# Attention backward on one core: K transposed by the DMA crossbar in place of TensorE

## The chip, the cores and the metric

The kernel runs on one core of a Trainium2 chip. Time is the device time of one launch in microseconds (us), taken over several runs; the profile is of one execution. The core has five engines that run side by side and wait for one another by semaphores: TensorE (PE in the profile; PEld are its weight loads), VectorE (DVE), ScalarE (ACT), GpSimd (POOL) and SyncE (SP, which here only issues DMAs). Transfers between HBM and SBUF, the on-chip memory of 128 partitions, run on 16 DMA engines. TensorE writes to PSUM, eight banks that DVE and ACT read.

## The reference

Two independent blocks, A and B, of multi-head attention over a given cache of keys and values, forward and backward. B = 8 batches, Sq = 96 queries, D = 640, H = 32 heads, Sk = 512 keys, Dh = 128; all bf16.

```python
def ref(x, k_cache, v_cache, wq, wo):              # once for A, once for B
    q = (x @ wq).reshape(B, Sq, H, Dh).transpose(0, 2, 1, 3)
    scores = einsum("bhqd,bhkd->bhqk", q, k_cache) * (Dh ** -0.5)
    p = softmax(scores, axis=-1)
    o = einsum("bhqk,bhkd->bhqd", p, v_cache)
    return o.transpose(0, 2, 1, 3).reshape(B, Sq, H * Dh) @ wo

out, vjp = jax.vjp(lambda *a: concatenate([ref(*a[:5]), ref(*a[5:])], -1), *inputs)
return out, *vjp(grad_out)     # gradients of x, k_cache, v_cache, wq, wo of A and B
```

The caches and their gradients are by far the largest arrays: 8 x 32 x 512 x 128 values each, for K, V, dK and dV of A and of B.

## The kernel before

The work is cut into **cells**: one head h and one batch b of one block, 2 x 32 x 8 = 512 of them. A cell brings in K and V of its head and batch (512 keys x 128, 128 KB each), and sends out dK and dV of the same size. Around the cells lies work per head (projections of Q and of the output gradient, `pA` to `pD`, and the gradients of wq and wo, `qA` to `qD`) and work per group of eight heads (`gU`, L480: output and dx summed over heads).

Every step is a function that is put on a list with a **tick** and a slot within the tick (`em.add`). Cell number n starts at tick n, and each of its steps has a fixed offset in ticks from there (`OFF`, L45). The list is sorted by tick and slot, and the steps are emitted in that order; a planner then orders the instructions on each engine, mostly as emitted. The steps S2 and S3 (scores, softmax) are under `tc.high_priority(2000)` and are placed earlier, as soon as what they read is there. Tiles have a fixed number of buffers (`bufs=`); an instruction that writes a tile waits until the last reader of the buffer is through.

The steps of a cell, with their ticks before the change:

- `c_ld` (tick 0): two DMAs from SP's queue load K_sb (11 buffers) and V_sb (8). Partition p gets keys 4p to 4p+3 (KC = 4 of them, 1 KB in one piece), so column block c of a tile holds keys 4p + c.
- `c_s1` (tick 2): TensorE transposes the four blocks of K and the four of V (L243, L245) into one PSUM bank, DVE copies the 1024 columns to SBUF as KVT (L247, 5 buffers); KT and VT are its halves.
- `c_s2a`, `c_s2b` (tick 3): scores S = Q K^T (L259), their maximum (DVE, L261), the exponential E with its row sum (ACT, L271).
- `c_s3a`, `c_s3b` (tick 3): reciprocal (L281) and P = E / sum (POOL, L290; 5 buffers).
- `c_s4`, first part of `c_s45` (tick 4): dV = P^T dO (L330), its copy (ACT, L332) to dV_sb (3 buffers), its store from SP's queue (L333); P transposed on TensorE (L313).
- second part of `c_s45` (tick 5): O^T = V^T P^T, which reads natural V (L306).
- `c_s6` (tick 6): dP = dO V^T, which reads VT (L352), and dS (DVE, L356).
- `c_s7`, first part of `c_s78` (tick 7): dK = dS^T Q (L394), its copy (ACT, L396) to dK_sb (3 buffers) and store (L397); dS transposed (L377).
- second part of `c_s78` (tick 8): dQ^T, which reads natural K (L370).

Natural K is thus read at ticks 2 and 8, natural V at ticks 2 and 5, KT at 3, VT at 6. The keys stand in the order (c, p) in every tile with a key axis; dS and P use the same order as the natural tiles, since they are multiplied with them.

Of the kernel before, what the change touches and what calls it, by code (L numbers as in the profile page):

```python
# [7 lines left out]
ACT = mybir.ActivationFunctionType  # L8
# [3 lines left out]
BF16 = mybir.dt.bfloat16  # L12
# [29 lines left out]
SL_GRP = 95  # L42
SL_SETUP = 96

OFF = dict(ld=0, s1=2, s2=3, s3=3, s4=4, s5=5, s6=6, s7=7, s8=8)  # L45
HK = dict(pA=-5, pB=-3, pC0=[-2, 0], pC1=[-1, 0], pD1=1, pD0=2, qA0=13, qA1=17, qB=[20, 17], qD=[(18, 0, 2), (19, 2, 5)])
EV = dict(pB0="act", pB1="dve", pC00="act", pC01="act", pC10="act", pC11="dve", pD0="dve", pD1="dve", qA0="dve", qA1="dve", qB0="act", qB1="act", qD="dve", gU="act")
GSPREAD0 = 9
# [2 lines left out]
SLOTS = dict(LOAD=0, S2A=5, S2B=5.5, S1=6, S8=10, S7=20, S5=30, S4=40, S6=50, S3A=52, S3B=53, S5B=54, HEAD=SL_HEAD, GRP=SL_GRP)  # L51


def build_block(tc, em, tick0, blk, x, kc, vc, wq, wo, g_all, out_all, dx, dk, dv, dwq, dwo, ident, ones, pools, HG=8, first=True, groups=None):
    nc = tc.nc
    B, Sq, D = x.shape
    _, H, Sk, Dh = kc.shape
# [5 lines left out]
    KC = Sk // 128  # L63
    scale = float(Dh) ** -0.5
# [27 lines left out]
    const, ps, kvp, wk, hd, hst, grp = (pools[k] for k in ("const", "ps", "kvp", "wk", "hd", "hst", "grp"))  # L92

    def bank(shape, dt, name):
        return ps.tile(shape, dt, name=name, tag="bank")
# [4 lines left out]
    CS = pools["CS"]  # L100
# [12 lines left out]
    def setup_T(which_, c):  # L113
        def f():
            key = "xT" if which_ == 0 else "gT"
            if c == 0:
                S[key] = const.tile([128, DC, T], BF16, name=key, bufs=1)
            dst = S[key]
            if first:
                tmp = S["x_nat" if which_ == 0 else "g_nat"][:, :, c * 128:(c + 1) * 128]  # L120
            else:
                tmp = S.pop(("tmp", which_, c))
            for t0 in range(0, TT, 8):
                nt = min(8, TT - t0)
                pt = bank([128, 8 * 128], BF16, "tp_ps")
                for i in range(nt):
                    nc.tensor.transpose(pt[:, i * 128:(i + 1) * 128], tmp[:, t0 + i, :], ident[:])
                nc.vector.tensor_copy(dst[:, c, t0 * 128:(t0 + nt) * 128], pt[:, 0:nt * 128])
        return f

    def setup_nat(which_):
        def f():
            key = "x_nat" if which_ == 0 else "g_nat"
            src_flat = x_flat if which_ == 0 else g_flat
            t_ = const.tile([128, TT, D], BF16, name=key, bufs=1)
            (nc.sync if first else nc.gpsimd).dma_start(t_[:], src_flat.rearrange("(t p) d -> p t d", p=128))
            S[key] = t_
        return f
# [6 lines left out]
    for c in range(DC):  # L145
# [4 lines left out]
        em.add(tick0 - 7 + c, SL_SETUP, setup_T(1, c))  # L150
    em.add(tick0 + (-11 if first else B + OFF["s5"] - 2), SL_LOAD, setup_nat(1))
    em.add(tick0 + (-12 if first else B + OFF["s8"] - 2), SL_LOAD, setup_nat(0))

# [9 lines left out]
    def pA(h):  # L163
        def f():
            wo_h = hd.tile([128, D], BF16, name="wo_h", bufs=1)
            nc.gpsimd.dma_start(wo_h[:], wo[h * 128:(h + 1) * 128, :])
            wq_h = hd.tile([128, DC, 128], BF16, name="wq_h", bufs=1)
            with nc.allow_non_contiguous_dma(reason="per-head wq slice"):
                nc.gpsimd.dma_start(wq_h[:], wq_v[:, :, h * 128:(h + 1) * 128])
            HS[(blk, h)] = dict(wo_h=wo_h, wq_h=wq_h)  # L170
        return f
# [54 lines left out]
                evac(EV["pD%d" % which], dst[:, b0 * 128:(b0 + nb) * 128], n_ps[:, 0:nb * 128])  # L226
        return f

    def c_ld(h, b):
        def f():  # L230
            K_sb = kvp.tile([128, KC, 128], BF16, name="K_sb", bufs=11)
            V_sb = kvp.tile([128, KC, 128], BF16, name="V_sb", bufs=8)
            nc.sync.dma_start(K_sb[:], kc[b, h].rearrange("(p c) d -> p c d", c=KC))
            nc.sync.dma_start(V_sb[:], vc[b, h].rearrange("(p c) d -> p c d", c=KC))
            CS[(blk, h, b)] = dict(K_sb=K_sb, V_sb=V_sb)
        return f

    def c_s1(h, b):
        def f():
            st = CS[(blk, h, b)]  # L240
            kvT_ps = bank([128, 2 * Sk], BF16, "kvT_ps")
            for c in range(KC):
                nc.tensor.transpose(kvT_ps[:, c * 128:(c + 1) * 128], st["K_sb"][:, c, :], ident[:])  # L243
            for c in range(KC):
                nc.tensor.transpose(kvT_ps[:, Sk + c * 128:Sk + (c + 1) * 128], st["V_sb"][:, c, :], ident[:])  # L245
            KVT = wk.tile([128, 2 * Sk], BF16, name="KVT", bufs=5)
            nc.vector.tensor_copy(KVT[:], kvT_ps[:])  # L247
            st["KT"] = KVT[:, 0:Sk]
            st["VT"] = KVT[:, Sk:2 * Sk]
        return f  # L250

    def c_s2a(h, b):
# [12 lines left out]
    def c_s2b(h, b):  # L265
        def f():
            with tc.high_priority(PRIO_OFF):
                st = CS[(blk, h, b)]
                E_sb = wk.tile([Sq, Sk], BF16, name="E_sb", bufs=2)
                rowsum = wk.tile([Sq, 1], F32, name="rowsum", bufs=3)  # L270
                nc.scalar.activation(E_sb[:], st["S_ps"][:], ACT.Exp, bias=st["negm"][:], scale=1.0, accum_out=rowsum[:])  # L271
                st["E_sb"], st["rowsum"] = E_sb, rowsum
                del st["S_ps"]
        return f
# [223 lines left out]
    for g in range(NG):  # L498
        h0 = GH0[g]
        for hh in range(groups[g]):  # L500
            h = h0 + hh
            c0t = tick0 + h * B
            em.add(c0t + HK["pA"], SL_LOAD, pA(h))
            em.add(c0t + HK["pB"], SL_HEAD, pB(h))
            for si in range(NTS):
                em.add(c0t + HK["pC0"][min(si, len(HK["pC0"]) - 1)], SL_HEAD, pC(h, 0, si))
                em.add(c0t + HK["pC1"][min(si, len(HK["pC1"]) - 1)], SL_HEAD, pC(h, 1, si))
            em.add(c0t + HK["pD1"], SL_HEAD, pD(h, 1))
            em.add(c0t + HK["pD0"], SL_HEAD, pD(h, 0))
            for b in range(B):  # L510
                ct = c0t + b
                em.add(ct + OFF["ld"], SLOTS["LOAD"], c_ld(h, b))
                em.add(ct + OFF["s1"], SLOTS["S1"], c_s1(h, b))
                em.add(ct + OFF["s2"], SLOTS["S2A"], c_s2a(h, b))
                em.add(ct + OFF["s2"], SLOTS["S2B"], c_s2b(h, b))
                em.add(ct + OFF["s3"], SLOTS["S3A"], c_s3a(h, b))
                em.add(ct + OFF["s3"], SLOTS["S3B"], c_s3b(h, b))
                em.add(ct + OFF["s5"], SLOTS["S5B"], c_s5b(h, b))
                em.add(ct + OFF["s4"], SLOTS["S4"], c_s4(h, b))
                S45.setdefault(ct + OFF["s5"], [None, None, None])[0] = (blk, h, b)  # L520
                S45.setdefault(ct + OFF["s4"], [None, None, None])[1] = (blk, h, b)
                S45.setdefault(ct + OFF["s6"], [None, None, None])[2] = (blk, h, b)
                S78.setdefault(ct + OFF["s8"], [None, None])[0] = (blk, h, b)
                S78.setdefault(ct + OFF["s7"], [None, None])[1] = (blk, h, b)
                em.add(ct + OFF["s6"], SLOTS["S6"], c_s6(h, b))
                em.add(ct + OFF["s7"], SLOTS["S7"], c_s7(h, b))
            em.add(c0t + HK["qA0"], SL_HEAD, qA(h, 0))
            for di in range(len(dsplits)):
                em.add(c0t + HK["qB"][min(di, len(HK["qB"]) - 1)], SL_HEAD + 1, qB(h, di))
            em.add(c0t + HK["qA1"], SL_HEAD, qA(h, 1))  # L530
            qd_parts = HK["qD"]
            for (k_, c_lo, c_hi) in qd_parts:
                if c_lo < DC:
                    em.add(c0t + k_, SL_HEAD + 2, qD(h, c_lo, min(c_hi, DC)))
        cLg = tick0 + (h0 + groups[g] - 1) * B + B - 1
        gs0 = max(3, (GSPREAD0 * groups[g]) // HG)
        gs1 = max(3, (GSPREAD1 * groups[g]) // HG)
        em.add(cLg + OFF["s5"] - 2, SL_LOAD, gW(g))
        subs = [(0, t, gi) for t in range(TT) for gi in range(len(gsplits))] + [(1, t, gi) for t in range(TT) for gi in range(len(gsplits))]
        n_out = TT * len(gsplits)  # L540
        for i, (which, t, gi) in enumerate(subs):
            if which == 0:
                tk = cLg + OFF["s5"] + 2 + (i * gs0) // n_out
            else:
                tk = cLg + OFF["s8"] + 2 + gs0 - 3 + ((i - n_out) * gs1) // n_out
            em.add(tk, SL_GRP, gU(g, which, t, gi))
# [119 lines left out]
```

## Time and profile before

| | us |
|---|---|
| median of 3 runs (lowest, highest) | 1850.45 (1850.15, 1851.11) |
| the profiled execution, its span | 1848.8 |
| TensorE busy | 1818.4 |
| VectorE busy | 1518.6 |
| ScalarE busy | 1434.4 |
| GpSimd busy | 777.9 |

The profile page gives for every engine its busy time, and for every group of instructions (a line of the kernel, an engine, an operation) the count, the busy time, the mean duration of one, and the idle time of the engine before them with what ended it. Durations on TensorE overlap, since its matmuls are pipelined; a mean duration there is not what one instruction takes of the queue. The chain of waits follows the work that ended last back from the end: at each step to the instruction that released it, or to the one before it on its engine. Two kinds of stretch alternate in the trace: some 147 us in which cells run with the work per head alone, and some 84 us in which the sums over a group of heads run between them.

### The profile page before, as it was taken

What the parts mean: (1) busy time and instruction counts of PE and PEld (TensorE: products, weight loads), DVE (VectorE), ACT (ScalarE), POOL (GpSimd) and SP (SyncE); (2) the same over time, 40 slices, a digit from 0 to 9 for tenths busy, and PEclk for the clock granted to TensorE, in tenths of its full rate; (3) what the DMA queues carried; (4) which work ended last, traced back from release to release, by engine and by line L of the source; (5) the groups of instructions that cost most, each with busy time, mean ns of one, the idle gap of its engine ahead of it and who ended that gap; (6) DMA issues with size and microseconds to landing.
All of it is one profiled execution on the core that took longest, in us unless ns stands there. A gap on an engine that the chain in (4) does not pass through costs nothing.

```text
span 1848.8 us, 69797 instructions
## 1 busy us (share of the span) xinstructions
PE 1818.4 (98%) x26595; PEld 1571.4 (85%) x26744; DVE 1518.6 (82%) x3309; ACT 1434.4 (78%) x4041; POOL 777.9 (42%) x1378
## 2 busy tenths in 40 slices
PE   6999999999999999999999999999999999999998
PEld 5888888888888888888888888888888888888887
DVE  5888867888788887888878887678887888878885
ACT  4888877888668886788767888788876788767882
POOL 4444433444334443345455444334433444333435
PEclk9999999999999999999999999999999999999999
DMA  7666654666546655566575665456655566555652
GB/s 229 196 193 202 192 162 149 199 195 193 164 148 194 201 183 165 159 191 205 186 229 173 196 194 184 160 167 198 192 175 164 171 196 199 159 165 176 201 168 84
DMA packets 316688, 335.32 MB, mean 181 GB/s; under 512 B 38368, under 2 KB 302048, under 8 KB 316352
## 3 DMA queue, kind: packets, MB, share of 16 engines
q1 hardware_dynamic: 296480, 270.53, 46.2%
q0 software_dynamic: 19872, 60.32, 10.7%
q8 instruction: 210, 3.44, 0.8%
q14 instruction: 126, 1.03, 0.2%
HBM read 171.57 MB, written 159.12 MB: 179 GB/s over the span
## 4 chain that ended last, share of the span: by engine, by line
PE 95%; POOL 2%; issue 1%; DVE 1%; DMA 1%; ACT 0%; POOLq 0%; SPq 0%; ACTq 0%
PE q_ps L210 11%; PE o_ps L480 10%; PE dV_ps L330 6%; PE kvT_ps L243 6%; PE kvT_ps L245 6%; PE dK_ps L394 6%; PE dP_ps L352 6%; PE S_ps L259 6%; PE dwq_ps L445 6%; PE dwo_ps L425 5%; PE optp_ps L313 5%; PE dq_dst_ps L377 5%; PE optp_ps L306 5%; PE dq_dst_ps L370 5%; PE n_ps L225 3%; PE nat_ps L410 2%
## 5 line engine op out<-in xcount | busy, mean ns | idle before, releaser
L290 POOL TENSOR_SCALAR P_sb<-E_sb,rinv 96x512 bf16<-96x512 bf16 x512 | 354.2, 692 | 780.5 <-DVE rinv L281 775.2
L271 ACT ACTIVATE E_sb<-S_ps,negm 96x512 bf16<-96x512 f32 x512 | 349.1, 682 | 291.2 <-DVE negm L261 288.1
L356 DVE SCALAR_TENSOR_TENSOR dS_sb<-dP_ps,dl_ps,P_sb 96x512 bf16<-96x512 f32 x512 | 383.3, 749 | 108.1 <-PE dl_ps L354 103.1
L247 DVE COPY KVT<-kvT_ps 128x1024 bf16<-128x1024 bf16 x512 | 350.0, 684 | 70.7 <-PE kvT_ps L245 69.0
L261 DVE TENSOR_REDUCE negm<-S_ps 96x1 f32<-96x512 f32 x512 | 347.6, 679 | 35.8 <-PE S_ps L259 30.1
L332 ACT ACTIVATE dV_sb<-dV_ps 128x512 bf16<-128x512 f32 x512 | 313.3, 612 | 0.0
L396 ACT ACTIVATE dK_sb<-dK_ps 128x512 bf16<-128x512 f32 x512 | 300.5, 587 | 15.7 <-PE dK_ps L394 12.9
L319 ACT ACTIVATE PT_sb<-optp_ps 128x384 bf16<-128x384 bf16 x512 | 253.4, 495 | 0.0
L245 PE MATMUL kvT_ps<-ident,V_sb 128*128 128x128 bf16 x2048 | 198.0, 219 | 0.0
L394 PE MATMUL dK_ps<-Qnat_h,dS_sb 96*128 96x128 bf16 x2048 | 197.9, 219 | 0.0
L243 PE MATMUL kvT_ps<-ident,K_sb 128*128 128x128 bf16 x2048 | 197.9, 219 | 0.0
L330 PE MATMUL dV_ps<-dOnat_h,P_sb 96*128 96x128 bf16 x2048 | 197.9, 219 | 0.0
L259 PE MATMUL S_ps<-KVT,QT_h 128*96 128x512 bf16 x512 | 193.8, 379 | 2.2 <-DVE KVT L247 1.9
L352 PE MATMUL dP_ps<-KVT,dOT_h 128*96 128x512 bf16 x512 | 195.2, 381 | 0.0
L342 POOL TENSOR_TENSOR prod<-OT_h,dOT_h 128x96 bf16<-128x96 bf16 x512 | 186.2, 364 | 19.4 <-ACT OT_h L316 14.4
L243 PEld LDWEIGHTS <-K_sb 128*128 128x128 bf16 x2048 | 147.3, 98 | 36.9 <-issue 1.9
L379 DVE COPY dST_sb<-dq_dst_ps 128x384 bf16<-128x384 bf16 x512 | 175.4, 343 | 1.8 <-PE dq_dst_ps L377 0.8
L313 PE MATMUL optp_ps<-ident,P_sb 96*128 96x96 bf16 x2048 | 171.6, 205 | 2.3 <-POOL P_sb L290 2.0
L377 PE MATMUL dq_dst_ps<-ident,dS_sb 96*128 96x96 bf16 x2048 | 172.1, 206 | 0.5 <-DVE dS_sb L356 0.4
L306 PE MATMUL optp_ps<-PT_sb,V_sb 128*128 128x96 bf16 x2048 | 172.1, 206 | 0.0
L370 PE MATMUL dq_dst_ps<-dST_sb,K_sb 128*128 128x96 bf16 x2048 | 170.7, 206 | 0.0
L445 PE MATMUL dwq_ps<-dQnat,x_nat 128*128 128x128 bf16 x1920 | 143.2, 219 | 0.0
(84 smaller groups left out, 3949.8 us busy)
## 6 DMA issues: line engine op xcount, KB each, us to landing
out_dram<-dV_sb SPq DMA_DIRECT2D x512, 128.0 KB, 2.0
out_dram<-dK_sb SPq DMA_DIRECT2D x512, 128.0 KB, 2.3
K_sb<-in_A_k_cache_dram SPq DMA_DIRECT2D x256, 128.0 KB, 2.4
V_sb<-in_A_v_cache_dram SPq DMA_DIRECT2D x256, 128.0 KB, 2.5
K_sb<-in_B_k_cache_dram SPq DMA_DIRECT2D x256, 128.0 KB, 2.4
V_sb<-in_B_v_cache_dram SPq DMA_DIRECT2D x256, 128.0 KB, 2.5
out_dram<-dwq_sb POOLq DMA_DIRECT2D x64, 160.0 KB, 3.0
out_dram<-dwo_sb POOLq DMA_DIRECT2D x64, 160.0 KB, 2.7
```

What stands on the lines that cost most here:

```text
L243: nc.tensor.transpose(kvT_ps[:, c * 128:(c + 1) * 128], st["K_sb"][:, c, :], ident[:])
L245: nc.tensor.transpose(kvT_ps[:, Sk + c * 128:Sk + (c + 1) * 128], st["V_sb"][:, c, :], ident[:])
L247: nc.vector.tensor_copy(KVT[:], kvT_ps[:])
L259: nc.tensor.matmul(S_ps[:], hs["QT_h"][:, tok], st["KT"], start=True, stop=True)
L261: nc.vector.tensor_reduce(negm[:], S_ps[:], axis=AX.X, op=ALU.max, negate=True)
L271: nc.scalar.activation(E_sb[:], st["S_ps"][:], ACT.Exp, bias=st["negm"][:], scale=1.0, accum_out=rowsum[:])
L290: nc.gpsimd.tensor_scalar(P_sb[:], st["E_sb"][:], st["rinv"][:], 0.0, op0=ALU.mult, op1=ALU.add)
L330: nc.tensor.matmul(dV_ps[:, c * 128:(c + 1) * 128], P_sb[:, c * 128:(c + 1) * 128], hs["dOnat_h"][:, b * 128:(b + 1) * 128], start=True, s ...
L332: nc.scalar.activation(dV_sb[:], dV_ps[:], ACT.Identity, scale=1.0)
L352: nc.tensor.matmul(dP_ps[:], hs["dOT_h"][:, tok], st["VT"], start=True, stop=True)
L356: nc.vector.scalar_tensor_tensor(dS_sb[:], dP_ps[:], dl_ps[:, 0:1], st["P_sb"][:], op0=ALU.subtract, op1=ALU.mult)
L394: nc.tensor.matmul(dK_ps[:, c * 128:(c + 1) * 128], dS_sb[:, c * 128:(c + 1) * 128], hs["Qnat_h"][:, b * 128:(b + 1) * 128], start=True, s ...
```

## The change

K^T no longer comes from TensorE. A DMA transpose on SP's queue loads K a second time and writes it transposed to SBUF as KT (6 buffers, tick 0). It reads K of a cell as 16 rows of 32 keys (8 KB each) and puts out, for each of the 128 values of a key, 32 groups of 16: column 16 g + r of KT is key 32 r + g. The scores thus have their keys in another order, and the exponential of L271 reads them back in the order (c, p) by a rearranged access: for each c and each of the 16 rows r, eight values with a step of 64. Its output, and all after it, stand in the order of before.

V is still transposed by TensorE, now alone (VT, 512 columns), at tick 4 in place of 2. Natural V and natural K are loaded for two batches at a time (256 KB in one DMA; V2 with 5 buffers at tick 1 of the even batch, K2 with 4 at tick 5). Natural K is now read by dQ^T alone.

```diff
-OFF = dict(ld=0, s1=2, s2=3, s3=3, s4=4, s5=5, s6=6, s7=7, s8=8)
+OFF = dict(ldT=0, ldV=1, ldK=5, s1=4, s2=3, s3=3, s4=4, s5=5, s6=6, s7=7, s8=8)
...
-    def c_ld(h, b):
-        def f():
-            K_sb = kvp.tile([128, KC, 128], BF16, name="K_sb", bufs=11)
-            V_sb = kvp.tile([128, KC, 128], BF16, name="V_sb", bufs=8)
-            nc.sync.dma_start(K_sb[:], kc[b, h].rearrange("(p c) d -> p c d", c=KC))
-            nc.sync.dma_start(V_sb[:], vc[b, h].rearrange("(p c) d -> p c d", c=KC))
-            CS[(blk, h, b)] = dict(K_sb=K_sb, V_sb=V_sb)
+    def c_ldT(h, b):
+        def f():
+            KT = kvp.tile([128, Sk // 16, 16], BF16, name="KT", bufs=6)
+            nc.sync.dma_start_transpose(KT[:], kc[b, h].rearrange("(r g) d -> r (g d)", r=16))
+            CS.setdefault((blk, h, b), {}).update(KT=KT[:].rearrange("d g r -> d (g r)"))
+        return f
+
+    def c_ldV(h, b):
+        def f():
+            V2 = kvp.tile([128, 2, KC, 128], BF16, name="V2", bufs=5)
+            nc.sync.dma_start(V2[:], vc[b:b + 2, h].rearrange("b (p c) d -> p b c d", c=KC))
+            for i in range(2):
+                CS.setdefault((blk, h, b + i), {}).update(V_sb=V2[:, i])
+        return f
+
+    def c_ldK(h, b):
+        def f():
+            K2 = kvp.tile([128, 2, KC, 128], BF16, name="K2", bufs=4)
+            nc.sync.dma_start(K2[:], kc[b:b + 2, h].rearrange("b (p c) d -> p b c d", c=KC))
+            for i in range(2):
+                CS.setdefault((blk, h, b + i), {}).update(K_sb=K2[:, i])
         return f
 
     def c_s1(h, b):
         def f():
             st = CS[(blk, h, b)]
-            kvT_ps = bank([128, 2 * Sk], BF16, "kvT_ps")
+            vT_ps = bank([128, Sk], BF16, "vT_ps")
             for c in range(KC):
-                nc.tensor.transpose(kvT_ps[:, c * 128:(c + 1) * 128], st["K_sb"][:, c, :], ident[:])
-            for c in range(KC):
-                nc.tensor.transpose(kvT_ps[:, Sk + c * 128:Sk + (c + 1) * 128], st["V_sb"][:, c, :], ident[:])
-            KVT = wk.tile([128, 2 * Sk], BF16, name="KVT", bufs=5)
-            nc.vector.tensor_copy(KVT[:], kvT_ps[:])
-            st["KT"] = KVT[:, 0:Sk]
-            st["VT"] = KVT[:, Sk:2 * Sk]
+                nc.tensor.transpose(vT_ps[:, c * 128:(c + 1) * 128], st["V_sb"][:, c, :], ident[:])
+            VT = wk.tile([128, Sk], BF16, name="VT", bufs=5)
+            nc.vector.tensor_copy(VT[:], vT_ps[:])
+            st["VT"] = VT[:]
         return f
...
-                nc.scalar.activation(E_sb[:], st["S_ps"][:], ACT.Exp, bias=st["negm"][:], scale=1.0, accum_out=rowsum[:])
+                nc.scalar.activation(E_sb[:].rearrange("q (c r s) -> q c r s", c=KC, r=16), st["S_ps"][:].rearrange("q (s c r) -> q c r s", c=KC, r=16), ACT.Exp, bias=st["negm"][:], scale=1.0, accum_out=rowsum[:])
...
-                em.add(ct + OFF["ld"], SLOTS["LOAD"], c_ld(h, b))
+                em.add(ct + OFF["ldT"], SLOTS["LOAD"], c_ldT(h, b))
+                if b % 2 == 0:
+                    em.add(ct + OFF["ldV"], SLOTS["LOAD"], c_ldV(h, b))
+                    em.add(ct + OFF["ldK"], SLOTS["LOAD"], c_ldK(h, b))
```

## The prediction

> **What bounds the kernel now.** I read the page first: its busy shares, then the chain that ended last.
>
> ```profile
> span 1848.8 us, 69797 instructions
> PE 1818.4 (98%) x26595; PEld 1571.4 (85%) x26744; DVE 1518.6 (82%) x3309; ACT 1434.4 (78%) x4041; POOL 777.9 (42%) x1378
> PE 95%; POOL 2%; issue 1%; DVE 1%; DMA 1%; ACT 0%; POOLq 0%; SPq 0%; ACTq 0%
> ```
>
> TensorE is busy in 98% of the span and is 95% of the chain, so what counts is how long its queue is and whether it ever stands still. How much a group of its instructions holds the queue is not their mean duration (219 ns, pipelined), but the step in the chain of waits in order of time (start, length, what):
>
> ```profile
> 804.97 0.22 PE kvT_ps L243 x4
> 805.19 0.22 PE kvT_ps L245 x4
> 805.41 0.17 PE dq_dst_ps L370 x4
> ```
>
> Four transposes of K (L243) take 0.22 us of the queue, and so do the four of V (L245). An average over the span mixes two stages, so I took a stretch of each. In the windows below the columns after the length are PE, PEld, DVE, ACT and POOL busy, granted clock, DMA share, GB/s; the second fence is the same two windows for the score matmul of L259 alone, whose count is the number of cells (one head and one batch).
>
> ```profile
> 314.00:461.00 147.00, 146.37 (x2228) 126.09 (x2238) 129.76 (x284) 126.33 (x359) 64.70 (x117) 1.00 0.62 195
> 461.00:545.00 84.00, 83.63 (x1163) 73.15 (x1169) 65.48 (x146) 53.52 (x147) 27.61 (x48) 1.00 0.49 154
> ```
>
> ```profile
> 314.00:461.00 147.00, 17.39 (x46) 5.60 (x46) 1.00 0.62 195
> 461.00:545.00 84.00, 7.21 (x19) 2.33 (x19) 1.00 0.49 154
> ```
>
> In the **plain stage** a cell takes 147/46 = 3.20 us, of which ACT works 126.33/46 = 2.75, DVE 129.76/46 = 2.82, and the DMA engines 0.62 x 3.20 = 1.98. In the **group stage** (the projections of L480 run between cells) it takes 84/19 = 4.42 us, ACT 2.82, DVE 3.45, DMA 0.49 x 4.42 = 2.17. The two windows are 231 us for 65 cells; 512 cells are 7.88 such periods, 1820 us, and the other 29 us are start and tail. TensorE stands still for 0.63 us of the 147, so it is the bound in both stages, at full granted clock (1.00).
>
> **The change, part by part.**
>
> *TensorE.* Of the eight transposes of a cell four go, with their weight loads: 0.22 us x 512 = 113 us off the queue. Nothing is added on it. What is late next is read below.
>
> *DVE.* The copy out of PSUM halves from 1024 to 512 columns.
>
> ```profile
> L247 DVE COPY KVT<-kvT_ps 128x1024 bf16<-128x1024 bf16 x512 | 350.0, 684 | 70.7 <-PE kvT_ps L245 69.0
> L159 DVE COPY dQnat<-nat_ps 128x768 bf16<-128x768 bf16 x64 | 34.8, 544 | 0.0
> L379 DVE COPY dST_sb<-dq_dst_ps 128x384 bf16<-128x384 bf16 x512 | 175.4, 343 | 1.8 <-PE dq_dst_ps L377 0.8
> ```
>
> Between 384 and 768 columns a column costs (544 - 343)/384 = 0.52 ns, so 512 columns cost 343 + 128 x 0.52 = 410 ns, 0.27 us less. DVE has been off the bound and gets further from it: nothing is gained directly.
>
> *ACT.* The exponential of L271 reads the scores in another order (steps of 64 values in PSUM, eight at a time) and writes densely.
>
> ```profile
> L271 ACT ACTIVATE E_sb<-S_ps,negm 96x512 bf16<-96x512 f32 x512 | 349.1, 682 | 291.2 <-DVE negm L261 288.1
> L332 ACT ACTIVATE dV_sb<-dV_ps 128x512 bf16<-128x512 f32 x512 | 313.3, 612 | 0.0
> ```
>
> Every PSUM read of this trace is dense, so the price is unknown: below, the dense copy of as many values (612 ns, a gain of 0.07 us, if the exponential itself were free); above, a doubling of the 682 ns, my estimate for every value costing two. I take 0, the L271 row, whose count of values is unchanged, and keep +0.68 for a rival.
>
> *How far ACT lets the gain through.* A plain cell of 3.20 - 0.22 = 2.98 us asks 2.75 of ACT (92%, now 86%), 2.55 of DVE (86%, now 88%). If none of ACT's 0.45 us of idleness in a plain cell could shrink, that stage would gain nothing: 46/65 of 113 us = 80 us lost. If all could, nothing is lost. DVE at 88% now costs TensorE 0.63 us in 147, nearer the lower end, and several cells are in flight at once; I take 12 us of the 80.
>
> *DMA, added.* 512 crossbar loads of 128 KB, 67 MB more. What a load costs the 16 engines comes from the queues and issues:
>
> ```profile
> q1 hardware_dynamic: 296480, 270.53, 46.2%
> q0 software_dynamic: 19872, 60.32, 10.7%
> K_sb<-in_A_k_cache_dram SPq DMA_DIRECT2D x256, 128.0 KB, 2.4
> wo_h<-in_A_wo_dram POOLq DMA_DIRECT2D x32, 160.0 KB, 3.1
> wq_h<-in_A_wq_dram POOLq DMA_DIRECT2D x32, 160.0 KB, 3.4
> ```
>
> SP's queue q1 held all engines for 46.2% of 1848.8 = 854 us, for 270.53 MB: 3.16 us per MB, 0.41 us for 128 KB. That is the lower end. No row shows a crossbar. The upper end: a load of runs of 256 bytes (wq_h) lands 0.3 us after one of the same size in runs of 1280 (wo_h), for 512 runs more; in the diff's layout 16 values of 2 bytes, one from each row, come to lie together, 4096 pieces of 32 bytes where the plain load has 128 runs, and 3968 more at that price are 2.3 us, 2.7 in all. I take 0.5 us: same bytes, same queue, source rows of 8 KB, longer than the 1 KB runs of the plain load, and 1 KB written per partition as before. DMA is then 1.98 + 0.5 = 2.48 us of a 2.98 us cell, 83%, and 2.67 of 4.20 in a group cell: hidden behind TensorE. What it costs if it is not, the rivals work out.
>
> Here the Trainium skill speaks with two voices. "Advanced Engine Details and Errata", section X-Bar Transpose (TRN2), has crossbar loads as fast as regular ones: by it 0.41 us, and the sum below stands. "VectorE: DVE Perf Modes", section The three transpose paths, gives 1309 ns for a 128x128 crossbar transpose against 390 ns on TensorE; four one after another would be 5.2 us a cell, an estimate, and over 2600 us in all. The 0.22 us for four in this trace shows that its TensorE figure is a latency and no step, and its DMA figure may be one too; no run here shows it.
>
> *SP's queue and the buffers.* SP issues four DMAs a cell now and four after (a transpose, half of two pair loads, two stores).
>
> ```profile
> 805.61 0.34 SPq L233 DMA_DIRECT2D K_sb<-in_A_k_cache_dram  x1
> 827.87 2.05 SPq L234 DMA_DIRECT2D V_sb<-in_A_v_cache_dram  x1
> SPq L233 <- PE dq_dst_ps L377: 398.2, 381, 2.4
> SPq L333 <- ACT dV_sb L332: 237.6, 335, 9.4
> out_dram<-dV_sb SPq DMA_DIRECT2D x512, 128.0 KB, 2.0
> out_dram<-dK_sb SPq DMA_DIRECT2D x512, 128.0 KB, 2.3
> ```
>
> An issue holds SP 0.34 us, at worst 2.05. Three plain ones leave 2.98 - 1.02 = 1.96 us for the transpose's issue; I take 0.34, and by the worst row SP would be just full. The stores of dV and dK (L333, L397) queue behind it, and ACT waits for them only when the third buffer of dV_sb or dK_sb is still out: two cells, 6 us, against landings of 2.0 and 2.3 us. SP's waits for a free K buffer (398 us) cost TensorE nothing now, because the load is early. After it K^T is issued 3 ticks before the scores (9 us), natural K 3 before dQ, V 3 before its transposes, with free buffers from six, eight and ten cells back; a pair load of 256 KB by the 2.4 us row twice over is 5 us. If that cover went, each late load would stop TensorE by the difference. No DMA wait of a cell is on the chain today. Start and tail keep their shape: 0, within 5 us either way.
>
> **The sum.** 1848.8 - 113 + 12 = 1748 us of span. The three runs' median is 1850.45, 1.65 above this execution's span, so 1750 us.
>
> **The rivals.**
>
> *The crossbar is the bound (slower).* Place: the plain stage's DMA time. With c for one transpose, from c = 1.0 us on (1.98 + 1.0 = 2.98) it eats into the gain, and the decisive point is where 46 plain cells of 1.98 + c and 19 group cells of 4.20 make 231 us again: c = 1.31 us, three times the plain load. At c = 1.42 a plain cell takes 3.40, a group cell its 4.20: 236 us a period, +41 us, about 1890. If a transpose holds the queue for as long as a plain load takes to land (2.4 us), cells take 4.38 and 4.57: 288 us a period, +450 us, 2300. For it: nothing in the trace shows the crossbar, and the upper end is 2.7. Against it: q0, which carries the short runs, pays 197.8/60.32 = 3.28 us per MB, hardly more than q1's 3.16. This is also where the skill's 1309 ns would end. Chance 0.25.
>
> *The plain stage gains little.* Either its idleness doesn't shrink, or stores land late behind transposes and it waits for dV_sb: up to 80 of the 113 us go, 1775 to 1818; with a crossbar of 1.0 to 1.31 us, which ends in the same place, up to 1846. For it: 92% is a load that no long stretch shows now. Against: the DVE row. Chance 0.14.
>
> *The reordered read doubles the exponential (slower).* ACT then needs 3.43 us a plain cell: 46 x 3.43 + 19 x 4.20 = 237.6 us a period, +52 us, 1902; from +0.23 us a cell ACT is the bound there, from +0.54 the whole is slower than before. Chance 0.06.
>
> *No change within 0.2%* (some 4 us, what a measurement here can tell) by several of these at once: 0.05. That the transposes would not go is no rival: the diff leaves none of K on TensorE.
>
> **How the numbers follow.** Forecast 0.50 (its own range 1735 to 1775), little gain in the plain stage 0.14, crossbar 0.25, read order 0.06, no change 0.05. Faster 0.50 + 0.14 = 0.64, same 0.05, slower 0.31. Range: below, the whole 113 us and 5 from the start, 1732 (0.02 under it); above, c = 1.42, 1890, which leaves out some 0.15 of the crossbar's 0.25 and 0.03 of the read order's. Together 0.20.
>
> **What would show it.** Right: TensorE still over 95% busy; L245 in steps of 0.22 us with no L243; a plain cell near 3.0 us; VT copies near 410 ns; L271 near 682 ns; crossbar engine time near 0.5 us each, DMA below 90%. Wrong: a wait of L259 for the KT load (crossbar), ACT waiting for dV_sb or dK_sb stores (queue), L271 over 0.9 us (read order), or a DMA share near 1 in plain stretches, which would make the whole prediction wrong.

## The result and the profile after

| | before | after |
|---|---|---|
| median (lowest, highest), us | 1850.38 (1850.15, 1851.11) | 1805.23 (1800.59, 1806.63) |
| span of the profiled execution, us | 1848.8 | 1804.9 |
| mean cell, first three eighths of a period, us | 4.23 | 4.06 |
| mean cell, last five eighths, us | 3.14 | 3.09 |

The ratio is 0.975 (95% interval 0.9737 to 0.9764): 45 us faster, where 100 were forecast. The last two rows are the mean times from one score matmul to the next over the six middle periods of 64 cells (cells 64 to 447), cut into eighths: the group work falls into the first three, the other five are plain. A group cell has gained 0.17 of the 0.22 us that its transposes took, a plain cell only 0.05, so most of the loss lies in the plain stage.

The page of the changed kernel, with its busy shares, queues and the chain by engine:

```profile
PE 1743.5 (97%) x24696; PEld 1471.6 (82%) x24696; DVE 1408.6 (78%) x3309; ACT 1431.0 (79%) x4041; POOL 777.6 (43%) x1378
q1 hardware_dynamic: 312864, 337.67, 70.8%
q0 software_dynamic: 19872, 60.32, 13.9%
PE 66%; DVE 12%; DMA 9%; ACT 6%; issue 5%; POOL 2%; SPq 0%; ACTq 0%; POOLq 0%; DVEq 0%
```

TensorE is still busy 97% of the time, and by that line alone it would be the bound as before. The chain says otherwise: TensorE holds 66% of it in place of 95%, and DMA, which held 1%, holds 9%. Which DMAs these are, the chain in order of time shows; three of its longest pieces (start, length, what):

```profile
155.59 4.95 DMA out_dram<-dV_sb
167.91 4.33 DMA out_dram<-dV_sb
174.45 4.92 DMA out_dram<-dV_sb
```

They are stores of dV; stores of dK are among the others. A store is on the chain only if somebody waits for its buffer. The costliest groups (busy time and mean ns; after the second bar idle time of the engine just before them, and what ended most of it), and the waits of the engines (us, times, longest) name who:

```profile
L343 ACT ACTIVATE dV_sb<-dV_ps 128x512 bf16<-128x512 f32 x512 | 313.6, 613 | 36.1 <-DMA out_dram<-dV_sb 19.8
L407 ACT ACTIVATE dK_sb<-dK_ps 128x512 bf16<-128x512 f32 x512 | 302.6, 591 | 30.3 <-DMA out_dram<-dK_sb 22.4
L282 ACT ACTIVATE E_sb<-S_ps,negm 96x512 bf16<-96x512 f32 x512 | 350.2, 684 | 224.6 <-DVE negm L272 215.9
L259 DVE COPY VT<-vT_ps 128x512 bf16<-128x512 bf16 x512 | 212.6, 415 | 48.0 <-PE vT_ps L257 47.2
```

```profile
ACT dK_sb L407 <- DMA out_dram<-dK_sb: 22.4, 25, 2.5
ACT dV_sb L343 <- DMA out_dram<-dV_sb: 19.8, 21, 2.4
```

Before, the evacuation of dV (its copy out of its PSUM bank) stood at 0.0 us of idleness. Now ACT waits 46 times and 42 us for a store of dV or dK to leave its buffer. These 42 us are no sum of losses, since ACT can catch up after one; they show where to look. The timeline of ACT and TensorE around 180 us shows one such wait and who stands behind it (in brackets the idle time and its releaser):

```profile
179.45 0.60 ACT L343 ACTIVATE dV_sb<-dV_ps 128x512 bf16<-128x512 f32 x1 [1.46 <-DMA out_dram<-dV_sb]
180.10 0.33 PE L317 MATMUL optp_ps<-PT_sb,V_4057 128*128 128x96 bf16 x4 [1.07 <-ACT dV_sb L343]
```

ACT stands still for 1.46 us until a store has landed, then evacuates dV; TensorE stands still for 1.07 us until that is done, since its next output goes to a bank as well. Why are the stores late? The same stretch on SP's queue (start, us an issue holds SP):

```profile
180.45 0.53 SPq L344 DMA_DIRECT2D out_dram<-dV_sb  x1
181.07 0.39 SPq L247 DMA_DIRECT2D K_4761<-in_A_k_cache_dram  x1
181.55 0.45 SPq L408 DMA_DIRECT2D out_dram<-dK_sb  x1
182.09 0.38 SPq L344 DMA_DIRECT2D out_dram<-dV_sb  x1
182.57 1.10 SPq L232 DMA_TRANSPOSE KT<-in_A_k_cache_dram  x1
183.76 0.53 SPq L239 DMA_DIRECT2D V_4958<-in_A_v_cache_dram  x1
184.39 0.42 SPq L408 DMA_DIRECT2D out_dram<-dK_sb  x1
```

SP never rests. Each issue begins some 0.1 us after the one before has ended, and a transpose holds SP for 1.10 us. All of them, by source line (shortest, median, longest ns), against the stores of before and after:

```profile
L232 SPq DMA_TRANSPOSE KT<-in_A_k_cache_dram x256: 1095/1101/4707, 1.8 to 864.3; - x128
L344 SPq DMA_DIRECT2D out_dram<-dV_sb x512: 332/529/1912, 30.5 to 1764.7; - x171
```

```profile
L333 SPq DMA_DIRECT2D out_dram<-dV_sb x512: 332/344/1640, 28.1 to 1808.6; - x171
```

The issue of a dV store has become longer too, 529 ns in place of 344. Over the last 24 cells of each of the six middle periods the issues take, per cell: transpose 1.25 us, the two stores 0.54 and 0.48, half a V pair 0.25, half a K pair 0.23, together 2.75. The gaps between them (0.09 in the median, four a cell) add 0.40, which makes 3.15 of a cell of 3.17 us: SP is full. From the end of an evacuation to the issue of its store there passed 0.03 us in the median before, and now 3.17 (dV) and 2.89 (dK); in those last 24 cells it is 4.2 to 4.7. With the landing the buffer is then out for 8.0 us in the median and for 11.6 at worst. The next evacuation into the same buffer is three cells on, and between the end of one and the start of the other lie 8.3 us where nothing waits. Of the 1024 evacuations 160 begin within 0.3 us of the landing of the store three cells back, and none did before.

Within a plain stretch the loss builds up. The eighths one by one, in us, are 3.90 4.41 3.87 2.97 2.99 3.11 3.13 3.26: the first plain cells run at the forecast 2.98, and then the queue has fallen behind.

The DMA engines look like a second suspect. A window of a plain stretch, columns as in the prediction, and the same for the score matmul alone:

```profile
50.00:200.00 150.00, 141.78 (x2044) 117.09 (x2044) 121.33 (x285) 128.62 (x370) 66.09 (x118) 1.00 0.94 233
```

```profile
50.00:200.00 150.00, 18.13 (x48) 5.83 (x48) 1.00 0.94 233
```

TensorE, which lost 0.63 us in 147, loses 8.2 in 150, and the DMA share is 0.94 where 0.83 was expected.

### The profile page after: what moved, and what is told of

The parts are those of the page before. It is cut to its first block, busy times and chain, and to the rows that moved or that the text cites. A ratio compares the mean times of both kernels' runs of the same rounds, so it can differ in the third digit from the quotient of the medians.

```text
span 1804.9 us, 65690 instructions
## 1 busy us (share of the span) xinstructions
PE 1743.5 (97%) x24696; PEld 1471.6 (82%) x24696; DVE 1408.6 (78%) x3309; ACT 1431.0 (79%) x4041; POOL 777.6 (43%) x1378
## 3 DMA queue, kind: packets, MB, share of 16 engines
q0 software_dynamic: 19872, 60.32, 13.9%
q14 instruction: 125, 1.02, 0.2%
## 4 chain that ended last, share of the span: by engine, by line
PE 66%; DVE 12%; DMA 9%; ACT 6%; issue 5%; POOL 2%; SPq 0%; ACTq 0%; POOLq 0%; DVEq 0%
PE q_ps L210 11%; PE o_ps L491 10%; PE dwq_ps L456 5%; PE S_ps L270 4%; PE dwo_ps L436 4%; PE vT_ps L257 4%; PE dK_ps L405 4%; PE dV_ps L341 4%; PE dP_ps L363 4%; DMA out_dram<-dK_sb 4%; DMA out_dram<-dV_sb 4%; DVE negm L272 3%; DVE dS_sb L367 3%; PE dq_dst_ps L381 3%; PE dq_dst_ps L388 3%
## 5 line engine op out<-in xcount | busy, mean ns | idle before, releaser
L259 DVE COPY VT<-vT_ps 128x512 bf16<-128x512 bf16 x512 | 212.6, 415 | 48.0 <-PE vT_ps L257 47.2
L270 PE MATMUL S_ps<-KT,QT_h 128*96 128x512 bf16 x512 | 193.5, 378 | 4.5 <-ACT dK_sb L407 2.2
L363 PE MATMUL dP_ps<-VT,dOT_h 128*96 128x512 bf16 x512 | 195.1, 381 | 2.8 <-ACT dV_sb L343 2.6
L292 DVE RECIPROCAL rinv<-rowsum 96x1 f32<-96x1 f32 x512 | 80.7, 158 | 94.4 <-ACT E_sb L282 81.2
L436 PE MATMUL dwo_ps<-g_nat,Onat 128*128 128x128 bf16 (+1 forms) x768 | 140.5, 299 | 0.7 <-ACT dK_sb L407 0.4
L210 PE MATMUL q_ps<-gT,woT_h 128*128 128x512 bf16 (+1 forms) x640 | 139.3, 325 | 0.1
L210 PE MATMUL q_ps<-xT,wq_h 128*128 128x512 bf16 (+1 forms) x640 | 131.3, 325 | 5.4 <-ACT E_sb L282 1.7
L456 PEld LDWEIGHTS <-x_nat 128*128 128x128 bf16 x1920 | 119.7, 98 | 20.3 <-issue 2.9
```

Source lines behind the costliest of these rows:

```text
L210: nc.tensor.matmul(q_ps[:], lhs(c), rhsT[:, c, t0:t0 + w], start=(c == 0), stop=(c == DC - 1))
L270: nc.tensor.matmul(S_ps[:], hs["QT_h"][:, tok], st["KT"], start=True, stop=True)
L363: nc.tensor.matmul(dP_ps[:], hs["dOT_h"][:, tok], st["VT"], start=True, stop=True)
L456: nc.tensor.matmul(w_ps[:, ci * 128:(ci + 1) * 128], S["x_nat"][:, t, c * 128:(c + 1) * 128], dQnat[:, t * 128:(t + 1) * 128], start=(t == ...
```

## The experiments

The theories that they tell apart: **A**, the crossbar transposes fill the DMA engines; **B**, they fill SP's queue, the stores are issued late, ACT waits for its buffers and TensorE for ACT; **C**, ACT has too little room in a plain cell, which explains the whole loss; **D**, the same for what is left of the loss when the crossbar is out of the way; **E**, the score's weight load, with which TensorE begins a score matmul, waits on a DMA; **F**, a transpose that waits for a free KT buffer holds up the stores behind it.

### The transfers alone

```diff
+        def tr(i, h):
+            nc.sync.dma_start_transpose(KT[i][:], kc[i % 8, h].rearrange("(r g) d -> r (g d)", r=16))
+
+        def ld(i, h):
+            nc.sync.dma_start(KN[i][:], kc[i % 8, h].rearrange("(p c) d -> p c d", c=4))
...
+        for i in range(N):
+            tr(i, i // 8)
...
+        for i in range(N):
+            ld(i, 8 + i // 8)
...
+        for i in range(N):
+            tr(i, 24 + i // 8)
+            ld(i, 24 + i // 8)
+            nc.sync.dma_start(dv[i % 8, i // 8].rearrange("(p c) d -> p (c d)", c=4), KN[(i + N // 2) % N][:].rearrange("p c d -> p (c d)"))
+            nc.sync.dma_start(dk[i % 8, 8 + i // 8].rearrange("(p c) d -> p (c d)", c=4), KN[(i + N // 2) % N][:].rearrange("p c d -> p (c d)"))
```

> Transfers alone, no arithmetic: 40 crossbar loads of 128 KB in a row, then 40 plain loads of the same size, then 40 pairs of both, then 40 cells' worth (crossbar load, plain load, two stores). Theory A (the crossbar holds the DMA engines for about 0.83 us, the 424 us that SP's queue gained over 512): 40 in about 33 us at a DMA share near 1, the plain ones in about 17 us. Theory B (the crossbar costs the engines what a plain load does, 0.41 us, and it is SP that is held 1.1 us for each): 40 in about 44 us, with a DMA share near 0.4. Theory C (ACT is too tight, the DMA doesn't matter): says nothing here.

From one execution: SP's timeline for 40 transposes and 36 plain loads one after the other, and the windows (length, POOL, clock, DMA share, GB/s) of transposes, of plain loads, and of cells of a transpose, a load and two stores:

```profile
0.73 50.61 SPq L576 DMA_TRANSPOSE KT<-in_A_k_cache_dram  x40
53.91 18.01 SPq L579 DMA_DIRECT2D KN<-in_A_k_cache_dram  x36
```

```profile
5.00:50.00 45.00, 0.00 (x0) 1.00 0.37 102
56.00:70.00 14.00, 0.00 (x0) 1.00 0.91 267
...
150.00:250.00 100.00, 0.00 (x0) 1.00 0.67 191
```

One transpose after the other takes 50.61/40 = 1.265 us, but keeps the engines busy for 0.37 of that: 0.47 us. A plain load takes 0.50 us at 0.91, 0.455 us of the engines. So the crossbar costs the engines what a plain load does, and SP 2.5 times the time. A transpose, a load and two stores take 2.71 us, and the engines are busy for 0.67 of it, 1.82 us: alone, this mix is bound by SP. That speaks for B, though 40 transposes took 51 us where B had 44: it had left out the gaps, and one transpose right behind another holds SP for 1.22 us and not for 1.10.

### A plain load in the transpose's place

```diff
-            nc.sync.dma_start_transpose(KT[:], kc[b, h].rearrange("(r g) d -> r (g d)", r=16))
+            nc.sync.dma_start(KT[:].rearrange("d g r -> d (g r)"), kc[b, h].rearrange("(p c) d -> p (c d)", c=KC))
```

> The changed kernel with each crossbar load replaced by a plain load of the same 128 KB into the same tile (the scores are then of untransposed keys); the order on TensorE, ACT and DVE is the same. Theory A (crossbar holds the DMA engines twice as long as a plain load): DMA share down from 0.86 to about 0.76, time 1745 to 1765 us. Theory B (SP held 1.1 us by each transpose): the same 1745 to 1765 us, since SP is free again. Theory C (ACT at 92% in the plain stage is what eats the gain): 1795 to 1810 us, no change.

1763.23 us (1762.69 to 1763.58), ratio 0.9524 (0.9509 to 0.9538): the lost time is the crossbar's. The same two windows of the plain stretch:

```profile
50.00:200.00 150.00, 147.40 (x2170) 123.95 (x2182) 129.19 (x303) 137.25 (x392) 70.80 (x127) 1.00 0.83 249
```

```profile
50.00:200.00 150.00, 19.02 (x51) 6.07 (x50) 1.00 0.83 249
```

There are 51 cells in place of 48, 2.94 us each, stores are issued 0.03 us after their data, and ACT, busy for 137 of 150 us (92%), stops nobody for long. So C falls as the whole cause. But both the engines and SP are relieved, so A and B both stand.

### Six store buffers in place of three

```diff
-            dV_sb = wk.tile([128, KC * 128], BF16, name="dV_sb", bufs=3)
+            dV_sb = wk.tile([128, KC * 128], BF16, name="dV_sb", bufs=6)
```

(The same for dK_sb.)

> The changed kernel with six buffers instead of three for dV_sb and dK_sb; the order of instructions is the same on every engine. Theories A and B (stores land late, ACT waits for a free buffer, TensorE behind it): 1755 to 1785 us, ACT's waits for the stores gone. Theory C: 1800 to 1810 us, no change.

1769.66 us (1768.6 to 1771.44), ratio 0.9557 (0.9541 to 0.9573) with every transpose in its place. Its plain stretch, and what is left of ACT's waits for stores:

```profile
50.00:200.00 150.00, 145.14 (x2143) 121.95 (x2152) 127.66 (x300) 135.44 (x386) 70.05 (x125) 1.00 0.97 233
```

```profile
ACT dV_sb L343 <- DMA out_dram<-dV_sb: 1.8, 2, 1.0
```

The stores are issued later than in the changed kernel (4.1 and 4.0 us after their data) and ACT hardly notices. The DMA engines are fuller than there, 0.97, and the kernel is 35 us faster: A cannot be the whole, and C is contradicted again, since ACT does the same work. A plain cell takes 2.98 us over the six middle periods, as with the plain load. Of the 7.7 us of span by which this kernel is still behind that one, 2 lie ahead of cell 6 and 3 in cells 48 to 64, where most of TensorE's waits for late loads of KT fall (3.5 us in the whole kernel).

### The stores from GpSimd's queue

```diff
-            nc.sync.dma_start(dv[b, h].rearrange("(p c) d -> p (c d)", c=KC), dV_sb[:])
+            nc.gpsimd.dma_start(dv[b, h].rearrange("(p c) d -> p (c d)", c=KC), dV_sb[:])
```

(The same for dk.)

> The changed kernel with the stores of dV and dK issued from GpSimd's queue and not from SP's. Theory A (the DMA engines are full): the stores still land late, 1795 to 1815 us. Theory B (they stand behind the transposes in SP's queue): 1750 to 1775 us. Theory C: 1800 to 1810 us. GpSimd's own issue time (0.6 to 0.9 us each in the trace of before) could make P_sb late and spoil the reading; its busy time would show it.

1775.76 us (1774.42 to 1782.24), ratio 0.9599 (0.9581 to 0.9616).

```profile
50.00:200.00 150.00, 147.31 (x2160) 123.46 (x2171) 129.16 (x303) 137.23 (x394) 126.16 (x227) 1.00 0.98 248
```

With three buffers and the engines at 0.98, a store goes out 0.30 (dV) and 0.46 us (dK) after its data, and most of the loss is gone. A falls as the cause of it. That it is some 6 us slower than with six buffers fits GpSimd's share of 76% in place of 43%, which was not tested by itself.

### SP held without a crossbar

On top of the plain load of K^T, two loads of 1 KB a cell that nobody reads:

```diff
-            nc.sync.dma_start_transpose(KT[:], kc[b, h].rearrange("(r g) d -> r (g d)", r=16))
+            [nc.sync.dma_start(kvp.tile([16, 32], BF16, name="pad", bufs=12)[:], kc[b, h, 0:16, 0:32]) for i in range(2)]; nc.sync.dma_start(KT[:].rearrange("d g r -> d (g r)"), kc[b, h].rearrange("(p c) d -> p (c d)", c=KC))
```

> The kernel of e2 (plain loads in place of crossbar loads) with two more DMAs on SP's queue ahead of each, of 1 KB each, which nobody reads: three issues of some 0.43 us with their gaps, as long as one transpose with its gap (1.25 + 0.09 us in the changed kernel), and next to no bytes. Theory B (SP's queue is full in the plain stage, so the stores are issued late): the loss comes back without any crossbar, 1790 to 1815 us, with stores issued microseconds after their data. Theory A (it is what the crossbar does to the DMA engines): 1760 to 1768 us, as e2.

1935.2 us (1931.71 to 1938.41), ratio 1.0454 (1.0438 to 1.047): the direction is B's, the size far over what was expected. ACT's waits:

```profile
ACT dK_sb L407 <- DMA out_dram<-dK_sb: 119.2, 99, 4.9
ACT dV_sb L343 <- DMA out_dram<-dV_sb: 42.7, 45, 2.5
```

It is the same wait, four times as long, with no transpose anywhere and a DMA share of 0.74 in the plain stretch. The stores go out 5.4 and 5.5 us late. Three issues of 0.47 us in the mean with three gaps hold SP for about 1.7 us, longer than one transpose with its gap. That explains the direction. It does not explain all of the size: some 40% of what this kernel loses against the plain load falls into group cells, where the stores go out some 10 us late in the median, and SP also has pauses in the middle of a cell, waiting for buffers. How much each costs was not taken apart. The granted clock was 0.983 to 0.99 here, against 0.999; if all of the time went with it, that would be some 30 of the 172 us.

### The pair loads undone

```diff
-            nc.sync.dma_start(V2[:], vc[b:b + 2, h].rearrange("b (p c) d -> p b c d", c=KC))
             for i in range(2):
+                nc.sync.dma_start(V2[:, i], vc[b + i, h].rearrange("(p c) d -> p c d", c=KC))
```

(The same for K2.)

> The changed kernel with each pair load of K and V issued as two loads of one batch, into the same tiles: the same bytes, one more issue a cell on SP (0.4 to 0.6 us). Theory B: a plain cell asks 3.15 + 0.5 = 3.65 us of SP, group cells (3.9 to 4.4 us) are not bound by it, so about 40 x 0.5 us a period of 64 cells: 1900 to 1980 us, slower than before. Theory A (bytes and engine time count): 1800 to 1815 us.

1962.56 us (1961.58 to 1964.65), ratio 1.0604 (1.0588 to 1.062). The bytes are unchanged, SP has one issue more a cell, and the kernel is 157 us slower than the changed one and 111 slower than before. From the second eighth of the plain cells on, a cell takes 3.64 us in the mean, where 3.65 was worked out from SP's issues. (The granted clock was 0.983 to 0.989; if all of the time went with it, that would be some 30 of the 157 us.)

```profile
ACT dK_sb L407 <- DMA out_dram<-dK_sb: 103.9, 109, 3.5
ACT dV_sb L343 <- DMA out_dram<-dV_sb: 81.9, 67, 3.1
```

Stores go out 6.0 and 6.2 us late. Without the merging of the loads, then, moving K's transposes would have made the kernel slower. One more instruction in a queue, with the same bytes: that speaks strongly for B.

### Six buffers, and the pair loads from GpSimd

The six store buffers, and `nc.gpsimd.dma_start` for V2 and K2.

> e3 (six store buffers) with the pair loads of K and V issued from GpSimd: SP has the transpose and two stores, 1.25 + 2 x 0.5 + 3 x 0.09 = 2.5 us of a 2.96 us cell. Theory B: stores issued within a few hundred ns of their data again, 1758 to 1768 us, the time of e2. Theory A (the DMA engines, 0.94 to 0.97 in e3's plain stage, hold it up): no better than e3, 1766 to 1775 us.

1769.84 us (1768.27 to 1771.67), ratio 0.9559 (0.9543 to 0.9575): no gain over six buffers alone, though stores go out 0.5 and 0.03 us after their data again. Its plain stretch, and one wait of TensorE at the start:

```profile
50.00:200.00 150.00, 146.43 (x2167) 123.43 (x2176) 129.25 (x304) 136.92 (x393) 106.80 (x176) 1.00 1.01 251
```

```profile
PE wqT_ps L184 <- DMA wq_h<-in_A_wq_dram: 5.5, 1, 5.5
```

B had 1758 to 1768 and just missed; A, with 1766 to 1775, had the time. But the place of the remainder decides between them. Seven of the 8 us of span between this kernel and the one with a plain load lie ahead of cell 8. There TensorE waits once for 5.5 us for a load of wq, which GpSimd issues and which it does not wait for in the kernel with the plain load; GpSimd now has the pair loads to issue as well. From cell 8 to cell 448 this kernel takes 1465.1 us and the one with a plain load 1464.0. With all transposes in place and the DMA engines at 1.01 (full, within what the profile resolves) the cells thus run as fast as without transposes: in the middle of the kernel nothing is left for A.

### What sets the time that a transpose holds SP

Twenty transposes each, of a cell in 16, 32, 64 and 128 rows, of half a cell (64 KB) and of two (256 KB), with nothing else:

```diff
+        for k, r in enumerate((16, 32, 64, 128)):
...
+            for i in range(N):
+                src = kc[i % 8, 4 * k + i // 8].rearrange("(r g) d -> r (g d)", r=r)
+                if r == 16:
+                    nc.sync.dma_start_transpose(KT[i][:], src)
...
```

> Crossbar loads alone, 20 of each shape: 16 rows of 8 KB, 32 of 4 KB, 64 of 2 KB, 128 of 1 KB (128 KB each), then 16 rows of 4 KB (64 KB) and 16 rows of 16 KB (256 KB). If SP pays by the tile of data, the four of 128 KB hold it 1.1 us each, the half 0.55 to 0.65 and the double some 2.1 us; if it pays by the instruction, all hold it near 1.1 us and a double one would halve the cost. A shape that holds SP shorter would be the one to use.

From one execution, SP's timeline with 16 rows, with 128, with 64 KB, and with 256 KB:

```profile
0.73 25.24 SPq L581 DMA_TRANSPOSE KT<-in_A_k_cache_dram  x20
85.75 21.15 SPq L587 DMA_TRANSPOSE KT<-in_A_k_cache_dram  x16
106.95 10.09 SPq L591 DMA_TRANSPOSE KTh<-in_A_k_cache_dram  x8
135.93 23.71 SPq L595 DMA_TRANSPOSE KTw<-in_A_k_cache_dram  x18
```

1.26, 1.32, 1.26 and 1.32 us each: SP pays for the instruction, not for its bytes or its shape. One transpose for two cells would halve the price. It was not tried in the kernel, where two cells that follow each other are two batches of one head, and these do not lie together in HBM.

### K^T without a DMA

```diff
-            nc.sync.dma_start_transpose(KT[:], kc[b, h].rearrange("(r g) d -> r (g d)", r=16))
+            nc.gpsimd.tensor_copy(KT[:].rearrange("d g r -> d (g r)"), CS[(blk, h, b)]["V_sb"].rearrange("p c d -> p (c d)"))
```

(V's load goes to tick 0, this copy to tick 2.)

> The changed kernel without any second load of K: GpSimd copies V from its natural tile into KT (the scores are then of untransposed V), natural V is loaded a tick earlier. SP has two stores and a pair load a cell, DMA is as before the change, and the order on TensorE and ACT is that of the changed kernel. It tests the rest of the gap, from e2 (1763 us) down to the forecast. Theory D (ACT at 91% of a plain cell): no change against e2, 1760 to 1768 us. Theory E (the weight load of the scores on TensorE now waits for a DMA's semaphore, and in some 95 of 512 cells the step behind the dl matmul is 0.25 us in place of 0.03): the steps of 0.25 us vanish and the time is 1735 to 1752 us. GpSimd works some 0.5 us more a cell.

1763.5 us (1762.02 to 1766.44), ratio 0.9526 (0.951 to 0.9542), the time of the plain load. With no second load of K at all nothing is gained. The wait that E is about, of the scores' weight load, here and with the plain load:

```profile
PEld L270 <- issue: 13.9, 83, 0.4
```

```profile
PEld L270 <- issue: 12.5, 76, 0.2
```

It is still there though no DMA can cause it, so E falls. D named the right time, but its reason is not shown: against the forecast a plain cell loses 0.07 us here and a group cell, where ACT is busy for 69%, still 0.05. What TensorE waits for is followed up below.

### Ten KT buffers

`name="KT", bufs=6` becomes `bufs=10`.

> The changed kernel with ten KT buffers in place of six; the order on TensorE, ACT, DVE and GpSimd is the same. Theory F (the transposes stand at the head of SP's queue waiting for a free KT buffer, and the stores behind them wait with them): 1765 to 1790 us. Theory B (SP is full with its own issues, whatever they wait for): 1795 to 1810 us.

1809.8 us (1807.12 to 1811.38), ratio 0.9777 (0.9762 to 0.9792): no gain, and ACT's waits remain.

```profile
ACT dV_sb L343 <- DMA out_dram<-dV_sb: 33.0, 31, 3.8
ACT dK_sb L407 <- DMA out_dram<-dK_sb: 18.7, 29, 2.2
```

F falls. The stores are late (3.28 and 3.07 us) because SP is busy, not because it waits.

## Where the prediction held and where it failed, step by step

**TensorE: right.** The four transposes of K made up 114.3 us of TensorE's queue before (from the start of the first to the start of the matmul behind them, summed over 512 cells), against 113 in the forecast, and they are gone. **DVE: right**, 415 ns a copy against 410. **The exponential: right.** The read in steps of 64 values takes 684 ns, and the dense one took 682; the rival in which it doubles has fallen.

**The crossbar's engine time: right, but other transfers grew longer beside it.** Alone a transpose costs 0.47 us, against 0.5 in the forecast. That bears out what the Trainium skill says in "Advanced Engine Details and Errata", section X-Bar Transpose (TRN2), that such loads are as fast as regular ones. In the kernel, q1 held the engines for 0.708 x 1804.9 = 1278 us, 424 more than before; over 512 transposes that would be 0.83 us each. The packet records of the trace say whose time it is. The transposes' source rows are its 8192 packets of 8 KB: 469 ns each, 240 us of the 16 engines, again 0.47 us per transpose. The rest is other packets: the 262144 of 1 KB, as many as before, took 59.5 ns each in place of 50.7, 145 us more, and those of 4 bytes 38 us more. With the plain load q1's time is worked out from these lines:

```profile
q1 hardware_dynamic: 362016, 337.64, 62.9%
q0 software_dynamic: 19872, 60.32, 11.2%
```

0.629 x 1761.8 = 1108 us, 0.50 us for each added load. The longer transfers made the plain stretch's DMA share 0.94 and not 0.83. The prediction had called a share near 1 in plain stretches a sign that would make all of it wrong; it was no bound, since with six buffers or GpSimd's stores the kernel ran at 0.97 and 0.98 and was 29 to 36 us faster, and with the pair loads from GpSimd at 1.01. So the rival "the crossbar is the bound" did not come about.

**SP's queue: this step failed.** The prediction had it as "Three plain ones leave 2.98 - 1.02 = 1.96 us for the transpose's issue; I take 0.34, and by the worst row SP would be just full." A transpose holds SP for 1.10 us in the median, 1.27 in the mean, and a plain issue for 0.48 to 0.54 us in this company, not 0.34; the 0.09 us between two issues were not counted at all. The sum is 3.15 us for a cell of 2.98, more than fits. (With its own worst row the step had 1.02 + 2.05 = 3.07, which is over the cell and not "just full".) The cover for the store buffers, on which the step relied, was 8.3 us and not the 6 that it put down, and even that went: stores were 4.2 to 4.7 us late at the end of a period, and took 3.3 to 3.6 to land in place of 2.0 and 2.3. The landing alone would have done no harm: with the plain load it is 3.3 us as well, and ACT waits for no store. Six buffers win back 35.4 us of span (1804.9 to 1769.5), and that is most of what the forecast missed. The mechanism stood in the text, as the half of the rival "The plain stage gains little" in which "stores land late behind transposes and it waits for dV_sb", at 1775 to 1818, where the result lies. It was weighed by ACT's load alone, which is what the other half of that rival rests on. SP's time was there to be added up, and its upper bound, 2.05 us, was already known to fill the queue: two values that far apart, with the outcome hanging on them, should not have been settled at the lower one.

Beside it stands the figure of 1309 ns that the Trainium skill gives for a crossbar transpose ("VectorE: DVE Perf Modes", section The three transpose paths). The prediction weighed it as four a cell, one after another. It lies near the 1.26 us from one transpose's issue to the next, which here is paid once an instruction on SP, whatever its size.

**What ACT lets through: the size was off.** The term was 12 us; 1848.8 - 113 = 1735.8, and the kernel with the plain load takes 1761.8, so 26 went. In TensorE's queue, measured from the start of one matmul to the next, they are mostly the step behind the small dl matmul (L365): 16 us before, and about 40 in the kernels with the plain load and with the GpSimd copy (512 steps added up). About a hundred cells take 0.25 us there, the others 0.03. One of them with the plain load, from the timeline:

```profile
401.44 0.16 PE L365 MATMUL dl_ps<-ones,prod 128*96 128x1 bf16 x1
...
401.46 0.19 ACT L282 ACTIVATION_READ_ACCUMULATOR E_sb<-S_ps,negm 96x1 f32 x1
...
401.70 0.22 PE L456 MATMUL dwq_ps<-dQnat,x_nat 128*128 128x128 bf16 x1
```

TensorE starts its next matmul right after ACT is through with the exponential. With the plain load 106 of these steps are longer than 0.2 us, and in 101 of them the semaphore that came last for the next matmul is that of the exponential's last instruction: TensorE waits for ACT there. Nearly all of these matmuls begin work per head (q_ps, dwq_ps). They read nothing that the exponential writes, so what they wait for is probably its PSUM bank, since the eight banks go round; before, K's transposes took 0.22 us in every round. This reading is from the trace alone. No run moved the bank or shortened ACT's work, so it stays open whether the order of the banks or ACT's load is to blame.

**Start, tail, loads: right.** KT lands 4.0 us after its issue, and scores hardly ever wait for it (0.4 us in all).

The account, in span: 1848.8 - 113 (transposes) + 26 (the steps that stood behind them) + 8 (what six buffers leave: the first cells and late KT loads) + 35 (SP's queue and three store buffers) = 1804.8, and 1804.9 was measured. The parts are differences of kernels, which add up to the measured span by construction; taken in another order, 8 and 35 might split otherwise.

## What to carry to other kernels

Add up the issuing queue's time per iteration as one does an engine's: every instruction by its own hold, and the gap between two; where a new instruction's hold is unknown and its upper bound fills the queue, price that case first. What queues last is hurt first: here stores behind loads, whose buffers then stop an engine that has room to spare, so a busy share of 79% is no evidence that this engine cannot be late. Merging loads or issuing from another queue relieves the queue, and more store buffers make the delay harmless: six in place of three give 1769.66 us, 4.4% under the kernel before and 2% under the changed one.

## What the hardware showed that was not expected

- A DMA transpose held SP for 1101 ns in the median in the changed kernel, behind plain issues, and for 1222 to 1279 ns alone and one behind the other; there the next followed at 1.25 to 1.32 us, with 64, 128 or 256 KB and with 16 to 128 rows.
- With the transfers alone, a plain load's issue right behind a transpose holds SP for 0.57 to 0.58 us; the stores of dV before, with no transposes on the queue, held it for 0.344 us in the median.
- With transposes in the kernel, other transfers take the engines longer. A packet of 1 KB took 52.9 ns with the plain load and 59.5 with transposes. q0 moves 60.32 MB in both: with the plain load it took 0.112 x 1761.8 = 197 us of the engines, with transposes 0.139 x 1804.9 = 251 us, 27% more. Why is open; transposes with nothing but plain loads and stores beside them showed no such rise (1.82 us for four, 0.455 each; 51.7 ns for a packet of 1 KB).
